# Four-index merge weights stored channel by channel, a new load order at the start, and new planner constants in a fused S4 convolution and gated-GLU kernel

## The chip, the cores and the metric

The kernel runs on one core of one Trainium2 chip. The metric is the device time of one execution in microseconds (us); lower is better. TensorE (PE) multiplies matrices, VectorE (DVE) and ScalarE (ACT) work on elements, and one queue on SyncE (SP) issues every DMA, in order. GpSimd (POOL) does nothing here.

## What is computed

`u` (2048 x 512) goes into two branches, and a gate per row mixes their results:

```python
g = _sigmoid((x * gate_w).sum(-1, keepdims=True))
# branch a: a long convolution per channel d, with a kernel K of length 2048
logdA = dt * A                     # A, B, C complex, 512 channels x 128 states
P = jnp.exp(logdA[:, :, None] * l[None, None, :])
K = jnp.einsum("dn,dnl,dn->dl", Cc, P, dB).real
y = irfft(rfft(u) * rfft(K)) + u * Dskip
# branch b: a gated linear unit, 512 -> 1792 -> 512
h = _sigmoid(x @ w_gate) * (x @ w_up)
b = h @ w_down
return g * a + (1 - g) * b
```

## The kernel before, in words

**Who orders the work.** Nothing is ordered by hand. `Plan` (L111) holds a set of generators ("strands"), one per stage. A strand yields steps (engine, assumed duration, function, what it depends on); `run` (L159) always takes the step with the smallest key, which is its possible start plus the strand's constant in `BIAS` (L49), plus a part of the cost of a change of mode (`CHANGE`, L51). The chosen step is written into the program and the plan's clocks move on. So the constants and the assumed durations fix the order of the instructions on each engine, and each engine then runs its list in that order. A buffer ("slot") is given to the next user when the plan has freed it.

**Branch b** (`load_x` L695, `load_w` L727, `split` L705, `hidden` L758, `post` L787, `down` L809, `add` L835). The rows are done in two halves of 1024, each in two tiles of 512 columns (`sb`); the 1792 hidden units are 14 blocks `f` of 128, in groups of 4, 4, 3, 3 (`GROUPS`). Every f32 operand is split into a rounded high part (ACT, L713) and a low part (DVE, L714), and three products replace one: a block needs 24 matmuls of 128x512 into `gups` (L776), then `sg` (ACT L791), the product (DVE L793), `h` high (ACT L797) and low (DVE L798). `down` multiplies a group's `h` into `dps` (L825), and `add` accumulates (L841, L845). In the first half each block is loaded in three pieces of 256 KB through the staging tiles `st` (four of them, L687), split, and also stored split to `wsp` (L754, L755); the second half reads it back from there. `gu` and `dnw` have four buffers each, and a buffer is free when the block's matmuls are done and its store has landed.

**Branch a, the kernel K.** 512 channels are 16 groups of 32. `bases` (L294) loads a group's parameters (`pg`, `dt`), makes the angles (L321 to L346) and with one exponential 21 real powers per channel (`ep`, L347): eight coarse ones, eight fine ones and five that double. The 64 merge weights `mg` of a channel are the products of coarse and fine (L353, two instructions of 1024 elements per group), the bases `bz` use the last five (L360). `tables` (L381) makes `T` by five doublings (L375 to L377) and `B` (L406 to L410), and `kps` (L427) multiplies them, 128 short matmuls. `T` and `B` have one buffer each. `first` (L436) transforms the result (`wps`, L455), evicts it (`kev`, L467) and stores two groups at a time to `a_k` (L471).

**Branch a, u and the passes.** `rows` (L482) loads 16 tiles `u` (L488), takes the gate's sum (`ju`, DVE L491), transforms (`ups`, L506), evicts and stores to `a_u` (L523). When all rows are done, the pool `early` is closed and `passes` (L541) goes through two column halves of 256: once the half's `a_k` is complete, 16 steps of `s2u`, `s2k` (L535), the products on DVE (L585 to L595), `ips` (L607), `ev` (L614) and a store to `b_s`. After the 16th step of a half, `finals` (L627) reads `b_s` back (`b_in`, L641), and eight `fps` (L654) are mixed into the output (L667, L674, with `al` loaded at L664).

Of the kernel before, what the change touches and what calls it, by code (L numbers as in the profile page):

```python
# [31 lines left out]
P = 128  # L32
# [15 lines left out]

BIAS = dict(x=-0.91, w=0.02, split=-0.1, rows=-0.2, urest=1.37, bases=0.28, tables=0.33, first=0.42, hidden=0.92,  # L49
            post=0.04, down=0.54, add=0.22, passes=-4.76, step=0.19, finals=0.41, last=0.41, const=1.21)  # L50
CHANGE = dict(ACT=0.5, PE=1)  # L51
EARLY = -0.48

# [57 lines left out]
class Plan:  # L111
# [38 lines left out]
    def cost(self, eng, n):  # L150

        if eng == "PE":
            mode, n = n
            return n + (0.1 if mode != self.last else 0.0)
        if eng == "ACT" and isinstance(n, tuple):
            return n[1] + (1.28 if n[0] != self.kind else 0.0)
        return n

    def run(self):  # L159
        while True:  # L160
# [23 lines left out]
            if eng is None:  # L184
                end = start
            elif eng == "SP":
                end = start + 0.4
                self.free[eng] = end
                self.dma = max(self.dma, end) + m / 280e3
                end = max(self.dma, end + 0.6) + 1.4  # L190
            else:
                c = self.cost(eng, m)
                self.busy[eng] = self.busy.get(eng, 0.0) + c
                end = start + c
                self.free[eng] = end
                if eng == "PE":
                    self.last = m[0]
                    end += 0.35
                else:
                    if isinstance(m, tuple):  # L200
                        self.kind = m[0]
                    end += 0.2
            fn = st[2][2]
# [5 lines left out]
def body(ctx, tc, xp, xt, prm, ldt, dsk, gw, wgu, wdn, c_wu, c_wf, c_wk, c_ww, c_pw, out):  # L209
# [84 lines left out]
    def bases():  # L294
# [3 lines left out]
        for gi in range(NG):  # L298
# [10 lines left out]
            tn = kp.tile([P, 32], I32, tag="tn", name="tn")  # L309
            ep = kp.tile([P, NP, 32], F32, tag="ep", name="ep")  # L310
            ex, mg = exs.tile("ex"), mgs.tile("mg")
# [4 lines left out]
            def first():  # L316
                V.tensor_tensor(aa, pg[:, 0:2], dg, op=OP.mult)
                V.tensor_scalar(aa[:, 1], aa[:, 1], 1 / (2 * math.pi), None, op0=OP.mult)
            t = yield "DVE", 2 * dve(64) + 0.15, first, [ta, tb]
            sh = [P, NP, 32]  # L320
            te = yield "DVE", dve(32 * NP), lambda: V.tensor_tensor(  # L321
                ep, aa[:, 0:1].to_broadcast(sh), pw[:, NA:, None].to_broadcast(sh), op=OP.mult), [t]
            t = yield "ACT", act(32), lambda: A.activation(tn, aa[:, 1], AF.Copy), [t]
# [25 lines left out]
            sh = [P, 16, 8, 8]  # L349
            m8, m1 = (ep[:, i:i + 8].rearrange("p a d -> p d a") for i in (0, 8))  # L350
            tm = max(t, te)
            for d in (slice(0, 16), slice(16, 32)):
                tm = yield "DVE", dve(1024), lambda: V.tensor_tensor(  # L353
                    mg[:, d].rearrange("p d (a b) -> p d a b", b=8), m8[:, d, :, None].to_broadcast(sh),
                    m1[:, d, None, :].to_broadcast(sh), op=OP.mult), [tm - 0.2]
            bzs, = yield BZ, 1
# [3 lines left out]
            t = yield "DVE", dve(320), lambda: V.tensor_tensor(  # L360
                bz[:, 0::2], trig, ep[:, None, 16:].to_broadcast([P, 2, 5, 32]), op=OP.mult), [t, te, bzs.t]
            ti = yield "ACT", act(160), lambda: A.activation(bz[:, 1], bz[:, 2], AF.Copy, scale=-1.0), [t]
# [3 lines left out]
    def double(dst, src, b, nd, e, t):  # L366

        n = 2 * nd * e
        sh = [P, nd, 2, e]
        slot, = yield T2, 1  # L370
        t2 = slot.tile("t2")[:, :n].rearrange("p (d c e) -> p d c e", c=2, d=nd)
        br = b[:, 0, :, None, None].to_broadcast(sh)

        sb = b[:, 1:3].rearrange("p u d -> p d u")[:, :, :, None].to_broadcast(sh)
        yield "DVE", dve(n), lambda: V.tensor_tensor(t2, src, sb, op=OP.mult), [t, slot.t]  # L375
        t = yield "DVE", dve(n), lambda: V.tensor_tensor(dst, src, br, op=OP.mult), [t]  # L376
        t = yield "DVE", dve(n), lambda: V.tensor_tensor(dst, dst, t2[:, :, ::-1], op=OP.add), [t]  # L377
        slot.free(t - 0.2)
        return t

    def tables():  # L381
        for gi in range(NG):
# [39 lines left out]
            def small():  # L422
                for s in range(8):
                    for c in range(2):
                        for jj in range(4):
                            ch = 8 * jj + s
                            mm(p[32 * jj:32 * jj + 32, s], T[:, ch, c], B[:, ch, c],  # L427
                               start=(c == 0), stop=(c == 1), tile_position=(0, 32 * jj), skip_group_check=True)
            t = yield "PE", ("128x32", 1.9), small, [t, tb, bank.t]
            tas.free(t)  # L430
# [47 lines left out]
    US, EVU, JU = (slots(ep, n, k, s) for n, k, s in (("u", 2, [P, D]), ("evu", 2, [P, 2, D]), ("ju", 1, [P, D])))  # L478
    gate = [Ev() for _ in range(NM)]
    rleft = [NM]  # L480

    def rows():  # L482
        yield E["wu"]
        yield E["gwb"]
        for t in range(NM):
            us, = yield US, 1
            u = us.tile("u")
# [15 lines left out]
            def mms():  # L503
                for jp in range(2):
                    r = slice(64 * jp, 64 * jp + 64)
                    mm(ph[jp], wu[r, jp], u[r], start=True, stop=True, tile_position=(64 * jp, 0))  # L506
            tp = yield "PE", ("64x128", 0.9), mms, [tu, E["wu"].t] + [b.t for b in banks]
            us.free(max(tp, te))
# [32 lines left out]
    def passes():  # L541

        yield E["rows"]
        early.__exit__(None, None, None)
        fp = ctx.enter_context(pool("fin"))
# [19 lines left out]
    def step(j, q, ww, wws, au, ak, s2, ta, tk):  # L565
# [37 lines left out]
        def inverse():  # L603
            for c in range(2):
                for i in range(2):
                    r = slice(64 * i, 64 * i + 64)
                    mm(pi[i], ww[r, 2 + c], y[r, c], start=(c == 0), stop=(c == 1), tile_position=(64 * i, 0))  # L607
        t = yield "PE", ("64x128", 3.4e-3 * w), inverse, [t] + [b.t for b in banks]
        ys.free(t)
# [34 lines left out]
    def last(j, m, b, s2, tb):  # L644
# [5 lines left out]
        def mms():  # L650
            for x in range(4):
                for jb in range(2):
                    r = slice(64 * jb, 64 * jb + 64)
                    mm(ph[jb][32 * x:32 * x + 32], wf[r], b[x // 2][r, x % 2], start=True, stop=True,  # L654
                       tile_position=(64 * jb, 32 * x), skip_group_check=True)
        tp = yield "PE", ("64x32", 3.4e-3 * w), mms, [tb, E["wf"].t] + [k.t for k in banks]
        for s in s2:
# [21 lines left out]
    def finished(t, te):  # L679
# [47 lines left out]
    def load_w():  # L727
        for half in range(2):
            for f in range(NF):
# [193 lines left out]
```

## Time and profile before

| what | before |
|---|---|
| median of 3 runs | 745.72 us (741.02 to 746.52) |
| the profiled execution, its own time | 748.5 us |
| its span from the first to the last instruction | 746.7 us |
| mean granted TensorE clock | 0.981 |
| busy: PE, DVE, ACT | 680.0, 590.0, 374.9 us |
| last `kps` starts | 581.1 us |
| first `s2k` of the second pass | 601.6 us |
| last `ips` starts | 700.8 us |

All times inside the execution count from the start of the span. A row of the groups gives line, engine, operation, out<-in, partitions x elements and count, then busy time and the mean of one in ns, then the idle time of the engine just before. A row of the timeline gives start, length, engine, line and what is worked on. A row of the windows gives a stretch, its length, the busy time (and count) of PE, PEld, DVE, ACT and POOL, the granted clock, the DMA share and GB/s. PE's busy time includes the modelled end of each matmul, so it is more than the matmuls' spacing.

### The profile page before, as it was taken

What the parts mean: (1) busy time and instruction counts of PE and PEld (TensorE: products, weight loads), DVE (VectorE), ACT (ScalarE), POOL (GpSimd) and SP (SyncE); (2) the same over time, 40 slices, a digit from 0 to 9 for tenths busy, and PEclk for the clock granted to TensorE, in tenths of its full rate; (3) what the DMA queues carried; (4) which work ended last, traced back from release to release, by engine and by line L of the source; (5) the groups of instructions that cost most, each with busy time, mean ns of one, the idle gap of its engine ahead of it and who ended that gap; (6) DMA issues with size and microseconds to landing.
All of it is one profiled execution on the core that took longest, in us unless ns stands there. A gap on an engine that the chain in (4) does not pass through costs nothing.

```text
span 746.7 us, 15212 instructions
## 1 busy us (share of the span) xinstructions
PE 680.0 (91%) x6176; PEld 490.9 (66%) x6176; DVE 590.0 (79%) x1043; ACT 374.9 (50%) x594; POOL 0.2 (0%) x4
## 2 busy tenths in 40 slices
PE   1979979899899999989999999999989999999986
PEld 0647657666687787867665656767757856676643
DVE  6687998989989999999998999999898334434323
ACT  4757576758746356647374737655343223222210
POOL 0000000000000000000000000000000000000000
PEclk9989999999999999999999999999999999999998
DMA  7970528771557129429357556844257465765376
GB/s 221 363 264 26 137 70 274 295 214 41 141 181 286 55 75 302 146 81 321 112 150 197 170 168 185 311 128 140 65 157 275 95 195 168 222 237 174 113 207 212
DMA packets 100486, 133.96 MB, mean 179 GB/s; under 512 B 42304, under 2 KB 65216, under 8 KB 96832
## 3 DMA queue, kind: packets, MB, share of 16 engines
q1 hardware_dynamic: 100416, 132.99, 55.8%
q8 instruction: 49, 0.80, 0.4%
q14 instruction: 21, 0.17, 0.1%
HBM read 79.48 MB, written 53.48 MB: 178 GB/s over the span
## 4 chain that ended last, share of the span: by engine, by line
PE 45%; DVE 22%; DMA 13%; ACT 12%; issue 5%; SPq 1%; DVEq 0%; ACTq 0%
PE gups L776 20%; PE dps L825 9%; DVE mg L353 6%; PE ips L607 4%; DMA au<-a_u 4%; PE s2u L535 4%; PE s2k L535 3%; DMA al<-acc 2%; DMA st<-wdn 2%; PE kps L427 2%; DVE gups L793 2%; DMA u<-xp 2%; PE ups L506 2%; ACT L345 2%; PE wps L455 1%
## 5 line engine op out<-in xcount | busy, mean ns | idle before, releaser
L776 PE MATMUL gups<-x,gu 128*128 128x512 f32 x1344 | 333.2, 399 | 4.0 <-DMA gu<-wsp 2.4
L776 PEld LDWEIGHTS gups<-x,gu 128*128 128x128 f32 x1344 | 251.7, 191 | 77.0 <-issue 18.9
L825 PE MATMUL dps<-dnw,h 128*128 128x512 f32 x672 | 178.6, 407 | 13.8 <-ACT h L797 9.1
L825 PEld LDWEIGHTS dps<-dnw,h 128*128 128x128 f32 x672 | 124.0, 191 | 61.5 <-issue 15.3
L793 DVE TENSOR_TENSOR gups<-gups,sg 128x512 f32<-128x512 f32 x56 | 39.1, 698 | 44.5 <-PE gups L776 37.8
L797 ACT ACTIVATE h<-gups 128x512 fp32r<-128x512 f32 x56 | 33.2, 593 | 74.8 <-DVE gups L793 74.8
L353 DVE TENSOR_TENSOR mg<-ep 128x1024 f32<-128x1024 f32 x32 | 65.3, 2055 | 6.7 <-ACT ep L347 6.6
L585 DVE TENSOR_TENSOR tt<-s2k,uf 128x512 f32<-128x512 f32 x32 | 22.1, 689 | 44.0 <-PE s2k L535 43.6
L791 ACT ACTIVATE sg<-gups 128x512 f32<-128x512 f32 x56 | 33.6, 599 | 33.8 <-PE gups L776 33.6
L574 ACT ACTIVATE uf<-s2u 128x512 f32<-128x512 f32 x32 | 19.0, 595 | 60.4 <-PE s2u L535 50.1
L377 DVE TENSOR_TENSOR T<-T,t 128x64 f32<-128x64 f32 (+4 forms) x80 | 46.4, 580 | 1.0
L375 DVE TENSOR_TENSOR t<-T,bz 128x64 f32<-128x64 f32 (+4 forms) x80 | 46.2, 578 | 1.2
L376 DVE TENSOR_TENSOR T<-T,bz 128x64 f32<-128x64 f32 (+4 forms) x80 | 46.1, 577 | 0.0
L845 DVE SCALAR_TENSOR_TENSOR acc<-dps,omg,acc 128x512 f32<-128x512 f32 x48 | 36.0, 749 | 10.7 <-PE dps L825 10.6
L798 DVE TENSOR_TENSOR h<-gups,h 128x512 fp32r<-128x512 f32 x56 | 38.6, 688 | 6.7 <-ACT h L797 6.5
L427 PE MATMUL kps<-B,T 128*32 128x64 f32 x2048 | 33.7, 225 | 7.5 <-ACT evu L517 5.1
L535 PE MATMUL s2u<-au,ww 128*64 128x256 f32 x256 | 34.6, 390 | 6.4 <-DMA au<-a_u 5.5
L614 ACT ACTIVATE ev<-ips 128x256 f32<-128x256 f32 x64 | 21.0, 381 | 38.6 <-PE ips L607 38.5
L467 ACT ACTIVATE kev<-wps 128x256 f32<-128x256 f32 x64 | 33.2, 665 | 14.3 <-PE wps L455 14.2
L427 PEld LDWEIGHTS kps<-B,T 128*32 128x32 f32 x2048 | 31.0, 114 | 13.5 <-issue 6.1
L506 PE MATMUL ups<-u,wu 64*128 64x512 f32 x64 | 23.8, 734 | 17.0 <-DMA u<-xp 15.3
L406 DVE TENSOR_TENSOR B<-ex,mg 128x1024 f32<-128x1024 f32 x32 | 38.2, 1219 | 0.0
(80 smaller groups left out, 717.5 us busy)
## 6 DMA issues: line engine op xcount, KB each, us to landing
wsp<-gu SPq DMA_DIRECT2D x14, 1024.0 KB, 6.6
gu<-wsp SPq DMA_DIRECT2D x14, 1024.0 KB, 8.6
a_u<-evu SPq DMA_DIRECT2D x32, 256.0 KB, 4.0
a_k<-kev SPq DMA_DIRECT2D x8, 1024.0 KB, 6.8
ww<-c_ww SPq DMA_DIRECT2D x32, 256.0 KB, 3.0
au<-a_u SPq DMA_DIRECT2D x32, 256.0 KB, 3.5
ak<-a_k SPq DMA_DIRECT2D x32, 256.0 KB, 4.6
b_s<-ev SPq DMA_DIRECT2D x32, 256.0 KB, 4.7
```

The lines of the kernel that those rows point to most:

```text
L353: tm = yield "DVE", dve(1024), lambda: V.tensor_tensor(mg[:, d].rearrange("p d (a b) -> p d a b", b=8), m8[:, d, :, None].to_broadcast(sh) ...
L375: yield "DVE", dve(n), lambda: V.tensor_tensor(t2, src, sb, op=OP.mult), [t, slot.t]
L376: t = yield "DVE", dve(n), lambda: V.tensor_tensor(dst, src, br, op=OP.mult), [t]
L377: t = yield "DVE", dve(n), lambda: V.tensor_tensor(dst, dst, t2[:, :, ::-1], op=OP.add), [t]
L406: yield "DVE", dve(1024), lambda: V.tensor_tensor(B[:, d, :, 32:], ex[:, d, :, :32], mg[:, d, None, 32:].to_broadcast(sh), op=OP.mult), [tb]
L427: mm(p[32 * jj:32 * jj + 32, s], T[:, ch, c], B[:, ch, c], start=(c == 0), stop=(c == 1), tile_position=(0, 32 * jj), skip_group_check=True)
L506: mm(ph[jp], wu[r, jp], u[r], start=True, stop=True, tile_position=(64 * jp, 0))
L535: mm(p[64 * kb_:64 * kb_ + 64, c], ww[:, kb_, 64 * c:64 * c + 64], a(kb_), start=True, stop=True, tile_position=(0, 64 * kb_), skip_group_ ...
L776: mm(p, gu[:, a, k, dc], x[:, b, dc], start=(dc + n == 0), stop=(dc == NC - 1 and n == 2))
L793: t = yield "DVE", dve(512), lambda: V.tensor_tensor(pu, pu, sg, op=OP.mult), [t, tu]
L798: t = yield "DVE", dve(512), lambda: V.tensor_tensor(h[:, 1], pu, h[:, 0].bitcast(F32), op=OP.subtract), [t]
L825: mm(p, h[:, a, 128 * s:128 * s + 128], dn[:, b], start=(f == f0 and n == 0), stop=(f == f0 + gn - 1 and n == 2))
```

## The change

Line numbers in this section's new lines are three to ten higher than before's.

- `ep` is stored as [channel][power] instead of [power][channel]. `mg` then reads its coarse weight with eight repeats and its fine weights as eight neighbours; before, neighbours of the innermost index lay 32 elements apart. The product that makes `ep` (L321) and `bz` (L360) read their operands the other way round accordingly.
- A tile of `u` is not planned to be loaded before 8.7 + 12.1 t us on the plan's clock (`PACE`).
- The four loads of x's second tile wait until the weights of block 3 are issued (`XLATE`).
- Four more staging tiles lie in the pool `early`; `passes` takes them before it closes the pool.
- `BIAS`, `CHANGE`, `EARLY` and some assumed durations and latencies are other numbers. The assumed duration of one `mg` instruction, 1.13 us, is the same.

```diff
-CHANGE = dict(ACT=0.5, PE=1)
-EARLY = -0.48
+CHANGE = dict(ACT=0.5, PE=2)
+XLATE = 3
+PACE = [8.7, 12.1]
+EARLY = 0.5
...
-            ep = kp.tile([P, NP, 32], F32, tag="ep", name="ep")
+            ep = kp.tile([P, 32, NP], F32, tag="ep", name="ep")
...
-            sh = [P, NP, 32]
+            sh = [P, 32, NP]
             te = yield "DVE", dve(32 * NP), lambda: V.tensor_tensor(
-                ep, aa[:, 0:1].to_broadcast(sh), pw[:, NA:, None].to_broadcast(sh), op=OP.mult), [t]
+                ep, aa[:, 0, :, None].to_broadcast(sh), pw[:, None, NA:].to_broadcast(sh), op=OP.mult), [t]
...
             sh = [P, 16, 8, 8]
-            m8, m1 = (ep[:, i:i + 8].rearrange("p a d -> p d a") for i in (0, 8))
+            m8, m1 = ep[:, :, 0:8], ep[:, :, 8:16]
...
             t = yield "DVE", dve(320), lambda: V.tensor_tensor(
-                bz[:, 0::2], trig, ep[:, None, 16:].to_broadcast([P, 2, 5, 32]), op=OP.mult), [t, te, bzs.t]
+                bz[:, 0::2], trig, ep[:, :, 16:].rearrange("p d k -> p k d")[:, None].to_broadcast([P, 2, 5, 32]), op=OP.mult), [t, te, bzs.t]
...
+    more = slots(ep, "se", 4, [P, 512])
...
         for t in range(NM):
+            yield None, 0.0, None, [PACE[0] + PACE[1] * t]
             us, = yield US, 1
...
         yield E["rows"]
+        yield more, len(more)
         early.__exit__(None, None, None)
...
+    ST += more
...
-    wstored = [Ev() for _ in range(NF)]
+    wstored, begun_w = [Ev() for _ in range(NF)], [Ev() for _ in range(NF)]
...
             for sb in range(2):
+                if (half, sb) == (0, 1):
+                    yield begun_w[XLATE]
                 xsl, = yield X_, 1
...
                     yield from split(wdn[f], dn[:, 0], dn[:, 1], *args)
+                    begun_w[f].set(0.0)
```

The new constants move instructions on every engine. Three places matter below.

DVE, from the last instruction on `steps` (which makes the step sizes) to the first instruction of group 0 of K (`aa`). Before, in part:

```order
L282 TENSOR_TENSOR steps<-steps 16x32
L714 TENSOR_TENSOR x<-st,x 128x512
L714 TENSOR_TENSOR gu<-st,gu 128x512
L714 TENSOR_TENSOR x<-st,x 128x512
L491 SCALAR_TENSOR_TENSOR ju,gl<-u,gwb 128x512
L714 TENSOR_TENSOR x<-st,x 128x512
L517 COPY evu<-ups 128x512
L714 TENSOR_TENSOR x<-st,x 128x512 x3
L491 SCALAR_TENSOR_TENSOR ju,gl<-u,gwb 128x512
...
L491 SCALAR_TENSOR_TENSOR ju,gl<-u,gwb 128x512
L317 TENSOR_TENSOR aa<-pg,dt 128x64
```

Now:

```order
L285 TENSOR_TENSOR steps<-steps 16x32
L723 TENSOR_TENSOR x<-st,x 128x512
L723 TENSOR_TENSOR gu<-st,gu 128x512 x2
L723 TENSOR_TENSOR dnw<-st,dnw 128x512
L723 TENSOR_TENSOR gu<-st,gu 128x512 x2
L723 TENSOR_TENSOR dnw<-st,dnw 128x512
L723 TENSOR_TENSOR gu<-st,gu 128x512 x2
L723 TENSOR_TENSOR dnw<-st,dnw 128x512
L320 TENSOR_TENSOR aa<-pg,dt 128x64
```

The second tile of x and the work on `u` have left this place; ten splits stand ahead of `aa`, all but one of weights.

PE, from the last `kps` to the first step of the second pass (`s2u`). Before:

```order
L427 MATMUL kps<-B,T 32x64 x64
L455 MATMUL wps<-wk,kst 64x64 x32
L776 MATMUL gups<-x,gu 128x512 x18
L455 MATMUL wps<-wk,kst 64x64 x32
L825 MATMUL dps<-dnw,h 128x512 x30
L776 MATMUL gups<-x,gu 128x512 x12
L535 MATMUL s2u<-au,ww 64x256 x4
```

Now:

```order
L430 MATMUL kps<-B,T 32x64 x64
L835 MATMUL dps<-dnw,h 128x512 x3
L786 MATMUL gups<-x,gu 128x512 x6
L458 MATMUL wps<-wk,kst 64x64 x32
L786 MATMUL gups<-x,gu 128x512 x24
L835 MATMUL dps<-dnw,h 128x512 x3
L786 MATMUL gups<-x,gu 128x512 x18
L540 MATMUL s2u<-au,ww 64x256 x4
```

The `wps` of the group before the last now stands ahead of the last `kps`, and 9 matmuls of branch b instead of 18 and a `wps` stand between the last `kps` and its own `wps`.

PE, the end of the program. Before:

```order
L825 MATMUL dps<-dnw,h 128x512 x12
L654 MATMUL fps<-b_in,wf 32x256 x8
L825 MATMUL dps<-dnw,h 128x512 x6
L654 MATMUL fps<-b_in,wf 32x256 x8
L825 MATMUL dps<-dnw,h 128x512 x12
L654 MATMUL fps<-b_in,wf 32x256 x8
```

Now:

```order
L786 MATMUL gups<-x,gu 128x512 x6
L660 MATMUL fps<-b_in,wf 32x256 x8
L786 MATMUL gups<-x,gu 128x512 x6
L660 MATMUL fps<-b_in,wf 32x256 x8
L835 MATMUL dps<-dnw,h 128x512 x30
```

The last 30 matmuls of `down` now follow the last `fps`. From the last `ips` to the end stand 150 matmuls of branch b, before 102. Ahead of the last `kps` stand 1614, before 1650. Ahead of the fourth `kps`, in turn, stand 537, before 474.

On SP the four loads of x's second tile now follow the twelve loads of blocks 0 to 3, the eight stores of these blocks follow, and then the first tile of `u`. Nine tiles of `u` come after the second batch of weight loads, before three.

More of the change, by code (lines that the diff above doesn't have):

```diff
@@ L46 @@
 BANKS = dict(gu=3, dn=2, xb=3)
-BIAS = dict(x=-0.91, w=0.02, split=-0.1, rows=-0.2, urest=1.37, bases=0.28, tables=0.33, first=0.42, hidden=0.92,
-            post=0.04, down=0.54, add=0.22, passes=-4.76, step=0.19, finals=0.41, last=0.41, const=1.21)
-CHANGE = dict(ACT=0.5, PE=1)
-EARLY = -0.48
+BIAS = dict(x=-3.75, w=0.38, split=0.4, rows=-0.13, urest=1.21, bases=0.28, tables=0.35, first=0.47, hidden=0.91,
+            post=0.08, down=0.69, add=0.25, passes=-1.77, step=0.28, finals=0.11, last=0.24, const=4.74)
+CHANGE = dict(ACT=0.5, PE=2)
+XLATE = 3
+PACE = [8.7, 12.1]
+EARLY = 0.5
 def constants():
@@ L153, in cost @@
             mode, n = n
-            return n + (0.1 if mode != self.last else 0.0)
+            return n + (0.0 if mode == self.last else 0.09 if self.last == "f" else 0.1)
         if eng == "ACT" and isinstance(n, tuple):
@@ L186, in run @@
             elif eng == "SP":
-                end = start + 0.4
+                end = start + 0.43
                 self.free[eng] = end
@@ L197, in run @@
                     self.last = m[0]
-                    end += 0.35
+                    end += 0.22
                 else:
@@ L201, in run @@
                         self.kind = m[0]
-                    end += 0.2
+                    end += 0.13
             fn = st[2][2]
@@ L354, in bases @@
                     mg[:, d].rearrange("p d (a b) -> p d a b", b=8), m8[:, d, :, None].to_broadcast(sh),
-                    m1[:, d, None, :].to_broadcast(sh), op=OP.mult), [tm - 0.2]
+                    m1[:, d, None, :].to_broadcast(sh), op=OP.mult), [tm - 0.13]
             bzs, = yield BZ, 1
@@ L377, in double @@
         t = yield "DVE", dve(n), lambda: V.tensor_tensor(dst, dst, t2[:, :, ::-1], op=OP.add), [t]
-        slot.free(t - 0.2)
+        slot.free(t - 0.13)
         return t
@@ L428, in small @@
                                start=(c == 0), stop=(c == 1), tile_position=(0, 32 * jj), skip_group_check=True)
-            t = yield "PE", ("128x32", 1.9), small, [t, tb, bank.t]
+            t = yield "PE", ("128x32", 1.83), small, [t, tb, bank.t]
             tas.free(t)
@@ L506, in mms @@
                     mm(ph[jp], wu[r, jp], u[r], start=True, stop=True, tile_position=(64 * jp, 0))
-            tp = yield "PE", ("64x128", 0.9), mms, [tu, E["wu"].t] + [b.t for b in banks]
+            tp = yield "PE", ("64x128", 0.96), mms, [tu, E["wu"].t] + [b.t for b in banks]
             us.free(max(tp, te))
@@ L607, in inverse @@
                     mm(pi[i], ww[r, 2 + c], y[r, c], start=(c == 0), stop=(c == 1), tile_position=(64 * i, 0))
-        t = yield "PE", ("64x128", 3.4e-3 * w), inverse, [t] + [b.t for b in banks]
+        t = yield "PE", ("64x128", 3.75e-3 * w), inverse, [t] + [b.t for b in banks]
         ys.free(t)
@@ L655, in mms @@
                        tile_position=(64 * jb, 32 * x), skip_group_check=True)
-        tp = yield "PE", ("64x32", 3.4e-3 * w), mms, [tb, E["wf"].t] + [k.t for k in banks]
+        tp = yield "PE", ("64x32", 0.5 / 256 * w), mms, [tb, E["wf"].t] + [k.t for k in banks]
         for s in s2:
```

## The prediction

> **What bounds the kernel now.** I read the page first, then the windows by stage, then who waits ahead of `kps`. On the page:
>
> ```profile
> span 746.7 us, 15212 instructions
> PE 680.0 (91%) x6176; PEld 490.9 (66%) x6176; DVE 590.0 (79%) x1043; ACT 374.9 (50%) x594; POOL 0.2 (0%) x4
> PE   1979979899899999989999999999989999999986
> DVE  6687998989989999999998999999898334434323
> ```
>
> PE looks like the bound, but its busy time counts modelled ends. DVE's 79% is an average too: its slices stand at 8 and 9 up to three quarters of the span and fall to 3 behind that. The windows, cut where the work changes, say the same:
>
> ```profile
> 0.00:75.00 75.00, 54.01 (x246) 37.73 (x250) 53.81 (x112) 46.45 (x74) 0.20 (x4) 0.95 0.63 218
> 75.00:561.00 486.00, 454.92 (x4611) 337.37 (x4603) 454.95 (x781) 288.31 (x435) 0.00 (x0) 0.99 0.54 170
> 602.00:705.00 103.00, 101.06 (x594) 66.74 (x590) 44.95 (x84) 26.23 (x60) 0.00 (x0) 1.00 0.56 183
> 705.00:746.70 41.70, 31.40 (x218) 19.04 (x216) 14.08 (x26) 2.99 (x5) 0.00 (x0) 0.91 0.67 202
> ```
>
> From 75 to 561 us DVE is busy 454.95 of 486 us, and PE as long: 31 us idle each. Which of them leads is seen where they meet, at the `kps`:
>
> ```profile
> 253.01 1.24 DVE T L377
> 254.38 2.00 PE kps L427 x128
> ...
> 579.41 1.22 DVE L377 TENSOR_TENSOR T<-T,t 128x1024 f32<-128x1024 f32 x1
> 581.12 1.99 PE L427 MATMUL kps<-B,T 128*32 128x64 f32 x128
> ...
> L427 PE MATMUL kps<-B,T x2048: 216/219/314, 74.3 to 582.9; 128*32 128x64 f32 x187
> ```
>
> `kps` starts within 0.1 and 0.5 us of the end of the doubling that it needs (253.01 + 1.24 and 579.41 + 1.22). PE has matmuls of branch b to fill in, and K waits for DVE. The sixteen `kps` run from 74.3 to 581.1, so 33.8 us a group, and after the last of them comes a tail that nothing shortens by itself: store `a_k`, 16 steps, finals. So the end is the time of the last `kps` plus the tail, and DVE sets the first, with PE close behind.
>
> **The change part by part.** The merge weights first, with the instructions nearest to their old and new forms; the number behind the busy time is the mean of one in ns.
>
> ```profile
> L353 DVE TENSOR_TENSOR mg<-ep 128x1024 f32<-128x1024 f32 x32 | 65.3, 2055 | 6.7 <-ACT ep L347 6.6
> L409 DVE TENSOR_TENSOR B<-mg,ex 128x1024 f32<-128x1024 f32 x16 | 19.5, 1218 | 0.0
> L376 DVE TENSOR_TENSOR T<-T,bz 128x128 f32<-128x128 f32 x16 | 4.6, 287 | 0.0
> L337 DVE TENSOR_TENSOR w<-pg,dt 128x64 f32<-128x64 f32 x16 | 3.5, 219 | 0.0
> L394 DVE TENSOR_TENSOR w<-w,ex 128x64 f32<-128x64 f32 x16 | 4.4, 274 | 0.6
> L375 DVE TENSOR_TENSOR t<-T,bz 128x64 f32<-128x64 f32 x16 | 4.2, 264 | 0.0
> L321 DVE TENSOR_TENSOR ep<-aa,pw 128x672 f32<-128x672 f32 x16 | 13.6, 850 | 0.0
> L360 DVE TENSOR_TENSOR bz<-ex,ep 128x320 f32<-128x320 f32 x16 | 11.6, 728 | 0.0
> L594 DVE TENSOR_TENSOR y<-tt 128x256 f32<-128x256 f32 x32 | 13.4, 420 | 0.0
> ```
>
> `mg` and L409 both make 1024 elements from two f32 tiles in SBUF, and L353 costs 837 ns more. What differs is the step: in L353 the fine weights lie 32 elements apart. L394 shows the same at 64 elements (one operand 76 elements apart): 274 against 219 ns in L337, 0.86 ns per element, against 0.82 here. The new `mg` reads runs of eight neighbours; L376's form of 128 elements has runs of two and already costs 287, no more than the straight line from 219 (64 elements) to 420 (256) gives, 286. So I price it at 1.22 us, bounds 1.22 and 2.055. That is 32 x 0.837 = 26.8 us less on DVE, all of it ahead of the last `kps`.
>
> `bz` now reads both operands with steps. L360 already pays for one: a plain instruction of 320 elements costs some 487 by the line from 420 at 1.05 ns per element, it takes 728. L375 at 64 elements steps in both of its inputs and costs 264, less than one step in L394. So I take 0; the upper bound is the same penalty again, 16 x 0.24 = 3.8 us. The Trainium skill, SBUF — State Buffer, section "Door 1: The DMA port swizzle", says that each access to a new 16-byte line pays; taken as one payment for each operand it would give those 3.8 us, and the trace's L375 does not show the second payment. `ep` changes which operand repeats, and `mg`'s own case is the only one where such a pattern was dear; its new innermost run is 21 neighbours, so 850 stays. `ep`'s exponential runs over the same 672 neighbours either way.
>
> How much of 26.8 us reaches the end? PE must do the same work in fewer us. By the count in the order, 36 matmuls fewer stand ahead of the last `kps`; at 7.10 us for 30 (below) that is 8.5 us less. The stretch from 75 shrinks by 27 to 459 us with 446 us of PE in it, 97% busy; 101.06 of 103 us in the second pass is 98%, so it can be done, but hardly a stall may be left. PE's share was 93.6% (454.92 of 486). I take the middle of that and 98%, 96%: 446 / 0.96 = 465, so 6 us are lost again. The bounds are 0 (at 98%) and 17 (at 93.6%, 476 us).
>
> The start:
>
> ```profile
> 10.40 0.18 DVE L282 TENSOR_TENSOR steps<-steps 16x32 f32<-16x32 f32 x1
> 12.74 2.08 PE L506 MATMUL ups<-u,wu 64*128 64x512 f32 x4 [12.74 <-DMA u<-xp]
> 19.34 5.91 PE L776 MATMUL gups<-x,gu 128*128 128x512 f32 x18
> 24.58 0.22 DVE L317 TENSOR_TENSOR aa<-pg,dt 128x64 f32<-128x64 f32 x1
> L714 DVE TENSOR_TENSOR gu<-st,gu 128x512 fp32r<-128x512 f32 x28 | 18.7, 687 | 4.2 <-ACT gu L713 4.0
> ```
>
> K's first instruction, `aa`, came at 24.58. Now ten splits stand between the end of `steps` (10.58) and `aa`: 10 x 0.687 = 6.9 us, so 17.5 if the loads keep up, which eight staging tiles instead of four are for. That is 7 us earlier on DVE. PE begins with `gups` near 13 instead of two tiles of `u`, but the first `kps` stands behind 39 matmuls more (9.2 us) and 6 `ups` less (0.52 each by the row, 3.1). I take 5 us of gain, bounds 0 and 8. What is late instead are the tiles of `u`: nothing needs `a_u` before the first pass, when eight groups of K are done.
>
> The tail:
>
> ```profile
> 588.45 1.16 PE L455 MATMUL wps<-wk,kst 64*64 64x64 f32 x64
> 589.54 7.10 PE L825 MATMUL dps<-dnw,h 128*128 128x512 f32 x30
> 601.60 1.08 PE L535 MATMUL s2k<-ak,ww 128*64 128x256 f32 x8 [0.30 <-DMA ak<-a_k]
> 700.79 1.13 PE L607 MATMUL ips<-y,ww 64*128 64x256 f32 x8
> 704.75 5.33 SPq L641 DMA_DIRECT2D b_in<-b_s  x8
> 734.59 2.56 SPq L641 DMA_DIRECT2D b_in<-b_s  x4
> 738.71 1.53 PE L654 MATMUL fps<-b_in,wf 64*32 64x256 f32 x16
> ```
>
> The last `wps` began 5.3 us after the end of the last `kps` (583.11). Now 9 matmuls, 2.1 us, stand between them: 3.2 us less for everything behind. The 16 steps (601.6 to 700.8, 6.2 us each, with DMAs to and from DRAM in each) hold 198 matmuls of branch b, before 204: no change. The finals are bound by SP, which issues nearly without a pause from 704.75 to 737.15; PE is busy 31.40 of 41.70 us there, so the 48 matmuls more after the last `ips` fill idle time. But 30 of them now follow the last `fps`: 7.1 us, then the last sum and its store, where before the sum came right behind `fps`. Against that, one store less stands ahead of the last `b_in`, and the first of these 30 may overlap what `fps` waited for. I take +5, bounds 0 and +7.
>
> On the profiled execution: 748.5 - 26.8 + 6 - 5 - 3.2 + 5 = 724.5. That execution was 2.8 us above the median of the runs, so **721 us** in terms of the median, with the fraction dropped. Its own range, halfway to the bounds and all pulling together, is 714 (3 less lost, 1.5 more at the start, 2.5 less at the end) to 730 (5.5 more lost, 2.5 less at the start, 1 more at the end).
>
> **Rivals.** *DVE's other idle time goes too* (707): the 31 us that DVE idles from 75 on are partly waits for PE, whose order no longer runs into late tables; if 8 of them vanish and the 6 us above are not lost, 721 - 14. For it: L353 took 2.055 us where the plan assumed 1.13, so the plan reckoned with each table 1.8 us too early. Against: PE has no room for it, 97% being reckoned already.
>
> *PE paces* (739): if PE could not go faster, the relief of DVE is swallowed, and only the 36 matmuls that leave (8.5), the `wps` (3.2) and the end (+5) count: 748.5 - 6.7 - 2.8. For it: PE idles no more than DVE from 75 to 561. Against: the two rows of `kps` above.
>
> *The weights don't get cheaper* (742): if the price of `mg` hangs on its four indices with two repeats and not on the step, it stays at 2.055: 748.5 - 5 - 3.2 + 5 - 2.8. L375, L376 and L394 speak against it. The Trainium skill, VectorE: DVE Perf Modes, section "Mode 1× (REGULAR) — the baseline", goes this way: that mode assumes nothing, odd strides and f32 included, and gives one result per cycle. By that rule the layout is worth nothing; the trace disagrees, with 2055 against 1218 ns.
>
> *The tiles of u hold up PE* (753, slower). SP issues in order, and nine tiles of `u` now come after the second batch of weights, six more than before. There, stores to `wsp` stand ahead of them, which wait for splits, which wait for buffers; a late tile stops PE at its `ups`, and all matmuls behind.
>
> ```profile
> 158.83 8.78 DMA u<-xp
> PE ups L506 <- DMA u<-xp: 15.3, 2, 12.7
> ```
>
> The chain of before has one such load of 8.78 us. If six more cost PE 5.3 us each, 32 us, the gain is gone: 721 + 32. From about 4 us each the time is that of before. Against: PE waited 15.3 us in all for `u`, 12.7 of that at the very start, and two buffers let a load go ahead.
>
> **How the numbers follow.** Forecast 0.65, idle time goes too 0.13, PE paces 0.12, weights no cheaper 0.04, `u` holds up PE 0.06. A measurement of this kernel tells about 1%, 7.5 us, from no change, so faster means under 738.3: forecast, the first rival and half of the second, 0.84; within 1%: the other half and the third, 0.10; slower 0.06. The range, 702 to 739, holds the forecast, nearly all of the first rival and half of the second.
>
> **What would show it.** Right: `mg` near 1.22 us and `bz` near 0.73; `aa` near 17.5 us; the last `kps` near 555 us, still right behind its doubling; some 17 us from there to the first `s2k` of pass two; 42 to 49 us from the first `b_in` of pass two to the end. Wrong: `mg` above 1.5 us; or `kps` starting many us after its doubling (PE paces); or PE idle ahead of `ups` between 100 and 250 us, for more than 20 us in all. If the last `kps` comes after 570 us, the forecast fails whatever the total.

## The result, and the profile after

| what | before | after |
|---|---|---|
| median of 4 runs each | 745.18 us | 723.96 us (719.10 to 727.08) |
| ratio after / before | | 0.972 [0.965, 0.979] |
| the profiled execution, its own time | 748.5 us | 727.08 us |
| its span | 746.7 us | 725.3 us |
| first `kps` starts | 74.3 us | 66.0 us |
| last `kps` starts | 581.1 us | 554.9 us |
| first `s2k` of the second pass | 601.6 us | 573.3 us |
| last `ips` starts | 700.8 us | 670.7 us |

21 us are gone; 721 were forecast. First the page's totals and two of its rows of slices:

```profile
span 725.3 us, 15192 instructions
PE 678.0 (93%) x6176; PEld 491.3 (68%) x6176; DVE 567.9 (78%) x1045; ACT 374.6 (52%) x592; POOL 0.2 (0%) x4
PE   3999999999799969989999998998999999999987
DVE  6698999898999999898999998997996444443233
```

DVE did 22 us less than before, PE 2 us less. (Two copies of `evu` more run on DVE and take 1.3 us of its gain back.) The groups by form name the instruction that DVE's share comes from, and one that became dearer (mean ns behind the busy time):

```profile
L356 DVE TENSOR_TENSOR mg<-ep 128x1024 f32<-128x1024 f32 x32 | 38.3, 1220 | 4.1 <-ACT ep L350 4.0
L363 DVE TENSOR_TENSOR bz<-ex,ep 128x320 f32<-128x320 f32 x16 | 13.1, 821 | 0.0
L412 DVE TENSOR_TENSOR B<-mg,ex 128x1024 f32<-128x1024 f32 x16 | 19.5, 1220 | 0.0
```

`mg` went from 2055 to 1220 ns, to the ns what L412 takes, which also makes 1024 elements. `bz`, which now steps in both inputs, went from 728 to 821 ns.

The windows from the first `kps` to the end of the last, over the second pass, and over the finals (columns as before: stretch, length, busy time and count of PE, PEld, DVE, ACT, POOL, then clock, DMA share, GB/s):

```profile
66.00:557.00 491.00, 465.60 (x4979) 343.50 (x4979) 451.77 (x819) 295.16 (x455) 0.00 (x0) 0.98 0.57 184
573.00:672.00 99.00, 97.03 (x575) 63.26 (x576) 43.72 (x82) 24.18 (x56) 0.00 (x0) 1.00 0.56 187
672.00:725.30 53.30, 45.72 (x278) 30.58 (x277) 18.59 (x32) 5.20 (x10) 0.00 (x0) 0.97 0.51 163
```

Over the stretch of K, PE is the busier of the two: 94.8%, DVE 92.0%. Taken over the whole stretch, from the first `kps` to the end of the last, it was so before as well, 93.7% against 92.9%:

```profile
74.30:583.00 508.70, 476.42 (x4977) 353.96 (x4976) 472.69 (x815) 293.79 (x445) 0.00 (x0) 0.99 0.55 173
```

`kps` follows its doubling closely, as the timeline shows for the last group (start, length):

```profile
553.55 1.22 DVE L380 TENSOR_TENSOR T<-T,t 128x1024 f32<-128x1024 f32 x1
554.93 1.99 PE L430 MATMUL kps<-B,T 128*32 128x64 f32 x128
559.12 1.16 PE L458 MATMUL wps<-wk,kst 64*64 64x64 f32 x64
```

The doubling ends at 554.77, `kps` starts 0.16 us later, and the `wps` 2.2 us after `kps` has ended. Over the sixteen groups the first of these distances is 0.06 to 3.15 us, 1.1 in the mean; before it was 0.15 to 3.20, 1.2 in the mean. That alone does not show who waits. PE's idle time ahead of `kps`, in the groups of before and of after (the last part of each row), does:

```profile
L427 PE MATMUL kps<-B,T 128*32 128x64 f32 x2048 | 33.7, 225 | 7.5 <-ACT evu L517 5.1 <-DVE T L377 1.1 <-issue 0.9
L430 PE MATMUL kps<-B,T 128*32 128x64 f32 x2048 | 33.8, 225 | 7.4 <-DVE T L380 6.2
```

PE stood idle for the doubling 1.1 us in all before and 6.2 us after. At thirteen of the sixteen `kps` before, and at eleven after, it came straight from other matmuls.

The finals took longer than before, 54.6 us from the last `ips` against 45.9. SP's rows in the timeline of after, with the `o` that its stores wait for, the last matmuls and the last sum:

```profile
674.66 5.22 SPq L647 DMA_DIRECT2D b_in<-b_s  x8
...
687.66 2.90 SPq L677 DMA_DIRECT2D out<-o  x2
...
693.61 0.48 DVE L673 SCALAR_TENSOR_TENSOR o<-fps,g,al 128x256 f32<-128x256 f32 x1 [0.27 <-DMA al<-acc]
...
694.28 2.40 SPq L677 DMA_DIRECT2D out<-o  x2
...
696.73 0.42 SPq L670 DMA_DIRECT2D al<-acc  x1
697.24 2.55 SPq L647 DMA_DIRECT2D b_in<-b_s  x4
699.10 0.48 DVE L673 SCALAR_TENSOR_TENSOR o<-fps,g,al 128x256 f32<-128x256 f32 x1 [5.00 <-DMA al<-acc]
...
699.85 0.58 SPq L670 DMA_DIRECT2D al<-acc  x1
...
700.53 3.29 SPq L677 DMA_DIRECT2D out<-o  x2
702.97 0.48 DVE L673 SCALAR_TENSOR_TENSOR o<-fps,g,al 128x256 f32<-128x256 f32 x1 [2.72 <-DMA al<-acc]
...
708.67 2.56 SPq L647 DMA_DIRECT2D b_in<-b_s  x4
...
712.34 1.78 PE L660 MATMUL fps<-b_in,wf 64*32 64x256 f32 x16
714.05 7.49 PE L835 MATMUL dps<-dnw,h 128*128 128x512 f32 x30
721.57 0.75 DVE L855 SCALAR_TENSOR_TENSOR acc<-dps,omg,acc 128x512 f32<-128x512 f32 x1 [1.29 <-PE dps L835]
```

Two pairs of stores in the timeline of before, with what SP issues between them:

```profile
718.52 0.86 SPq L671 DMA_DIRECT2D out<-o  x2
...
719.43 0.93 SPq L664 DMA_DIRECT2D al<-acc  x2
...
720.46 2.55 SPq L641 DMA_DIRECT2D b_in<-b_s  x4
...
723.11 1.01 SPq L671 DMA_DIRECT2D out<-o  x2
```

A pair of stores held SP for 0.86 to 1.01 us before; now three of them hold it for 2.40 to 3.29 us. The cause for two of them, at 687.66 and 700.53, is SP's order. Before, it issues two `al`, then four `b_in`, then the two stores: the `al` land and the `o` are made largely while the `b_in` are issued. Now it issues one `al`, four `b_in`, one `al` and then the two stores: the second `al` stands directly ahead of the pair (699.85), `o` waits for it until 702.97, and the second store waits for that `o`. SP's waits for `o` over the loads of `b_in`, in before and in after (us in total, times, longest):

```profile
SPq L671 <- DVE o L667: 0.5, 1, 0.5
```

```profile
SPq L677 <- DVE o L673: 4.6, 2, 2.5
```

For the pair at 694.28 both `o` were made by 694.09, so it is something else that held SP there, and I do not know what. The next `al` and `b_in` stand behind each pair. From the first to the end of the last `b_in` it was 32.4 us and is 36.6; from there to the end 9.55 and now 14.07, and there the 30 matmuls are PE's last work.

### The profile page after: what moved, and what is told of

The parts are those of the page before. It is cut to its first block, busy times and chain, and to the rows that moved or that the text cites. A ratio compares the mean times of both kernels' runs of the same rounds, so it can differ in the third digit from the quotient of the medians.

```text
span 725.3 us, 15192 instructions
## 1 busy us (share of the span) xinstructions
PE 678.0 (93%) x6176; PEld 491.3 (68%) x6176; DVE 567.9 (78%) x1045; ACT 374.6 (52%) x592; POOL 0.2 (0%) x4
## 4 chain that ended last, share of the span: by engine, by line
PE 72%; DMA 10%; DVE 9%; ACT 4%; SPq 3%; issue 3%; DVEq 0%; ACTq 0%
PE gups L786 35%; PE dps L835 16%; DMA au<-a_u 4%; PE ips L613 4%; PE kps L430 4%; PE s2u L540 4%; PE s2k L540 3%; DMA u<-xp 3%; PE wps L458 2%; PE ups L511 2%; PE fps L660 2%; ACT kev L470 1%; DMA a_k<-kev 1%; DVE t L378 1%; DVE T L379 1%
## 5 line engine op out<-in xcount | busy, mean ns | idle before, releaser
L835 PE MATMUL dps<-dnw,h 128*128 128x512 f32 x672 | 176.7, 405 | 1.4 <-ACT h L807 0.9
L620 ACT ACTIVATE ev<-ips 128x256 f32<-128x256 f32 x64 | 21.4, 380 | 42.3 <-PE ips L613 42.3
L470 ACT ACTIVATE kev<-wps 128x256 f32<-128x256 f32 x64 | 33.5, 669 | 17.5 <-PE wps L458 17.4
L356 DVE TENSOR_TENSOR mg<-ep 128x1024 f32<-128x1024 f32 x32 | 38.3, 1220 | 4.1 <-ACT ep L350 4.0
L430 PE MATMUL kps<-B,T 128*32 128x64 f32 x2048 | 33.8, 225 | 7.4 <-DVE T L380 6.2
L613 PE MATMUL ips<-y,ww 64*128 64x256 f32 x256 | 36.3, 402 | 0.1
```

The lines of the kernel that those rows point to most:

```text
L356: tm = yield "DVE", dve(1024), lambda: V.tensor_tensor(mg[:, d].rearrange("p d (a b) -> p d a b", b=8), m8[:, d, :, None].to_broadcast(sh) ...
L430: mm(p[32 * jj:32 * jj + 32, s], T[:, ch, c], B[:, ch, c], start=(c == 0), stop=(c == 1), tile_position=(0, 32 * jj), skip_group_check=True)
L470: te = yield "ACT", 0.95, lambda: [A.activation(dst[:, :, i], src[:, :, i], AF.Copy) for i in range(2)], [t, kv.t]
L835: mm(p, h[:, a, 128 * s:128 * s + 128], dn[:, b], start=(f == f0 and n == 0), stop=(f == f0 + gn - 1 and n == 2))
```

## The experiments

Each ratio goes by runs of the kernel before on the same chip (its medians were 745.2 to 747.4 us); four runs of each kernel (old_layout seven), and the `kps` are those of the profiled one. "Ahead of the last `kps`" counts the matmuls of branch b that PE's order has there; behind it I give those after the last `kps`, the last `ips` and the last `fps`.

| kernel | median us | ratio [95%] | first / last `kps` | ahead; behind |
|---|---|---|---|---|
| before | 745.2 | 1 | 74.3 / 581.1 | 1650; 366, 102, 0 |
| after | 723.96 | 0.972 [0.965, 0.979] | 66.0 / 554.9 | 1614; 402, 150, 30 |
| new_layout | 731.0 | 0.980 [0.975, 0.984] | 71.9 / 566.6 | as before |
| old_layout | 740.7 | 0.995 [0.991, 0.999] | 68.4 / 571.1 | as after |
| less_dve | 724.5 | 0.969 [0.964, 0.975] | 66.9 / 552.3 | as after |
| less_pe | 722.5 | 0.969 [0.964, 0.974] | 64.0 / 549.6 | as after, but 1502 ahead |
| less_both | 715.1 | 0.960 [0.957, 0.963] | 63.7 / 543.9 | as after, but 1502 ahead |
| no_pace | 731.8 | 0.979 [0.973, 0.985] | 66.4 / 562.6 | 1614; 402, 150, 30 |
| no_more | 776.3 | 1.043 [1.036, 1.049] | 68.9 / 555.6 | 1422; 594, 327, 192 |
| no_xlate | 782.4 | 1.050 [1.045, 1.054] | 66.6 / 560.5 | 1422; 594, 327, 192 |
| old_consts | 780.4 | 1.049 [1.041, 1.056] | 81.9 / 626.6 | 1884; 132, 0, 0 |
| tail_act | 721.9 | 0.970 [0.967, 0.973] | 66.2 / 556.7 | as after |
| tail_pool | 726.0 | 0.974 [0.969, 0.979] | 67.3 / 556.3 | as after |
| wide_tail | 722.4 | 0.968 [0.964, 0.973] | 66.7 / 557.5 | as after |

**Layout and order apart.** *new_layout* is the kernel before with the five edits of the layout alone; *old_layout* is the changed kernel with them undone. The instructions of each engine stand in the order of before and of after.

```diff
-            ep = kp.tile([P, NP, 32], F32, tag="ep", name="ep")
+            ep = kp.tile([P, 32, NP], F32, tag="ep", name="ep")
...
-            m8, m1 = (ep[:, i:i + 8].rearrange("p a d -> p d a") for i in (0, 8))
+            m8, m1 = ep[:, :, 0:8], ep[:, :, 8:16]
```

> The kernel before with the new layout of ep alone, the order on every engine as before. DVE paces K: about 18 us less than 745, so 727, last kps near 562, and the rest of the gain belongs to the order. PE paces, or the gain is the new order's: 740 to 745.

> The changed kernel with ep in the layout of before, every engine's instructions in the same order as in the changed kernel. DVE paces K: mg is back at 2.055 us, 26.8 us more on DVE, of which 18 to 25 reach the end, so 724 + 21 = about 745, last kps near 577; bz falls from 0.821 to 0.728. PE paces: the time stays within 6 us of 724. The new order is what counts: also within 6 us of 724.

The groups by form of new_layout:

```profile
L353 DVE TENSOR_TENSOR mg<-ep 128x1024 f32<-128x1024 f32 x32 | 38.5, 1219 | 5.2 <-ACT ep L347 5.1
L360 DVE TENSOR_TENSOR bz<-ex,ep 128x320 f32<-128x320 f32 x16 | 13.1, 818 | 0.0
```

The same two of old_layout:

```profile
L356 DVE TENSOR_TENSOR mg<-ep 128x1024 f32<-128x1024 f32 x32 | 65.5, 2073 | 4.1 <-ACT ep L350 4.0
L363 DVE TENSOR_TENSOR bz<-ex,ep 128x320 f32<-128x320 f32 x16 | 11.7, 734 | 0.0
```

Both prices go with the layout, whatever the order. The layout alone brings 2.0% (1.6 to 2.5), 15 us; the order alone 0.5% (0.1 to 1.0), 4 us. The first `kps` comes 2.4 us earlier by the layout and 5.9 by the order, together the 8.3 of after; the last comes 14.5 us earlier by the layout, 10.0 by the order, 26.2 by both. Behind the last `kps` the order costs: 165.6 us to the end before, 164.1 in new_layout, 167.8 and 170.4 in old_layout and after. So most of the gain is the layout's; the order brings K forward and gives part of it back at the end. Both kernels went the way of the first theory, by less than it said: the last `kps` at 566.6 and not near 562, and at 571.1 and not near 577.

**Which engine holds K now.** Three kernels leave work out of after, in the slots where it stood: *less_dve* the last, longest sum of the doublings (16 x 1.22 us), *less_pe* one of three products of `down` in the first half (112 matmuls counted, some 25 us), *less_both* both.

```diff
-        t = yield "DVE", dve(n), lambda: V.tensor_tensor(dst, dst, t2[:, :, ::-1], op=OP.add), [t]
+        t = yield "DVE", dve(n), lambda: V.tensor_tensor(dst, dst, t2[:, :, ::-1], op=OP.add) if e < 16 else None, [t]
...
-                                for n, (a, b) in enumerate(((0, 0), (1, 0), (0, 1))):
+                                parts = ((0, 0), (1, 0), (0, 1))[:3 - (half == 0)]
+                                for n, (a, b) in enumerate(parts):
```

> The changed kernel without the addition that ends the last doubling of T, one DVE instruction of 1.22 us per group, 19.5 us in all; what is computed is then not K. DVE still paces: the last kps comes 12 to 18 us earlier than 554.9 and the time is 709 to 713. PE paces by now: the last kps moves by less than 6 us and the time is above 718.

> The changed kernel without one of three products in the first half's down projection, 112 matmuls of 0.227 us less on PE, 25 us, all ahead of the last kps; half of the rows then lack that product. DVE paces: the last kps comes at most 8 us earlier and the time is 716 to 724. PE paces: the last kps comes 15 to 25 us earlier and the time is 700 to 709.

> Both of the last two cuts in one kernel: 19.5 us less on DVE and 25 us less on PE ahead of the last kps (K lacks the last addition of T, half of the rows lack one product). The two engines share the pace and each alone was held by the other: the last kps comes 14 to 20 us earlier than 554.9 and the time is 704 to 711. Something else paces (ScalarE, the latency of a chain through all engines, the DMA queue): it stays above 718, as each cut alone did.

Windows over the stretch of K, of less_dve:

```profile
67.00:554.00 487.00, 464.19 (x4973) 341.13 (x4975) 434.68 (x804) 294.77 (x454) 0.00 (x0) 0.99 0.58 185
```

of less_pe:

```profile
64.00:551.00 487.00, 449.07 (x4856) 325.84 (x4858) 450.50 (x819) 295.29 (x455) 0.00 (x0) 0.98 0.58 185
```

and of less_both:

```profile
64.00:546.00 482.00, 446.23 (x4875) 322.81 (x4864) 434.63 (x804) 294.60 (x455) 0.00 (x0) 0.98 0.58 188
```

Taking 19.5 us from DVE alone brought the last `kps` 2.6 us forward, taking 25 us from PE alone 5.3; neither total can be told from after's, and the 2.6 us are hardly more than two executions of one order differ by (up to 2.5 us, below under the finals). Taking both brought 11.0 us, and this interval lies wholly under after's. So neither engine alone holds K: where one is relieved the other stands right behind. In less_dve the won time is seen ahead of `kps`: from the last instruction of the doubling to `kps` it takes 3.0 us in the mean, in after 1.1, and PE is at other matmuls meanwhile. The widest case, the tenth group:

```profile
356.20 1.22 DVE L379 TENSOR_TENSOR T<-T,bz 128x1024 f32<-128x1024 f32 x1
...
363.94 1.99 PE L430 MATMUL kps<-B,T 128*32 128x64 f32 x126
```

But 11 of some 20 us is not all either, and under the 14 to 20 that were expected. In less_both PE is busy 92.6% of the stretch and DVE 90.2%, both less than in after, so a part goes into waits between the two that a fixed order keeps.

**The other pieces.** *no_pace* loads `u` when the plan has a buffer, *no_more* does without the four staging tiles, *no_xlate* does not hold x's second tile back; the constants stay. *old_consts* has the structure of after with before's `BIAS`, `CHANGE`, `EARLY`, durations and latencies.

```diff
-            yield None, 0.0, None, [PACE[0] + PACE[1] * t]
...
-    more = slots(ep, "se", 4, [P, 512])
...
-        yield more, len(more)
...
-    ST += more
...
-                if (half, sb) == (0, 1):
-                    yield begun_w[XLATE]
```

And of old_consts, a part:

```diff
-CHANGE = dict(ACT=0.5, PE=2)
+CHANGE = dict(ACT=0.5, PE=1)
-EARLY = 0.5
+EARLY = -0.48
...
-                end = start + 0.43
+                end = start + 0.4
```

> The changed kernel without the set intervals for u. PE's order hardly differs (the counts ahead of the kps are within 9 matmuls of the changed kernel's). The pace is worth nothing by itself: 721 to 728. The even spacing of u is what keeps PE fed early: first kps later than 68 and 730 or more.

> The changed kernel without the four extra staging tiles. The order then puts 1422 matmuls ahead of the last kps and leaves 192 behind the last fps, as in the kernel with x's second tile at its old place. DVE bounds K from below: the last kps comes no earlier than 545 in spite of 44 us less work for PE ahead of it, and the time is 765 to 790, since PE ends last. PE paces K: the last kps comes near 515.

> The changed kernel with x's second tile loaded at its old place, ahead of most of the first weights; the planner then orders everything anew. The start's gain comes from this part: the first kps moves from 66.0 towards 72 and the time is 728 to 732. The start's gain comes from the paced u and the staging: the first kps stays within 2 us of 66 and the time within 4 us of 724.

> The changed kernel's layout, staging, pace and late second tile of x, with all planner constants of before. The order then puts 1884 matmuls of branch b ahead of the last kps and not 1614. PE holds K too: 270 matmuls of 0.227 us are 61 us, the last kps comes at 600 to 616, and with a tail of 160 the time is 760 to 778. DVE alone paces K, as the forecast had it: the last kps stays within 10 us of 555 and the time is 715 to 730.

The windows of no_more, from the first `kps` to the end of the last, and from there to the end:

```profile
69.00:557.50 488.50, 444.31 (x4837) 324.28 (x4836) 438.11 (x800) 288.49 (x444) 0.00 (x0) 0.95 0.55 172
560.00:772.80 212.80, 199.87 (x1120) 139.72 (x1111) 77.24 (x135) 40.34 (x84) 0.00 (x0) 1.00 0.52 168
```

The same two of old_consts:

```profile
82.00:628.50 546.50, 517.56 (x5195) 386.76 (x5195) 462.39 (x831) 301.09 (x456) 0.00 (x0) 0.98 0.51 166
628.00:776.70 148.70, 105.69 (x752) 59.93 (x740) 48.74 (x96) 26.08 (x59) 0.00 (x0) 0.83 0.58 177
```

These two show the balance from its ends. In no_more the plan put 192 matmuls fewer ahead of the last `kps`, some 45 us of PE, and it came at 555.6 all the same, so less work for PE does not bring it forward. That DVE holds it there is not shown: PE is busy 91.0% of that stretch and DVE 89.7%, both less than in after. The 192 then run behind the last `fps`, PE is busy 94% of the last 213 us, and the end comes 52 us later. In old_consts 270 more stand ahead, PE is busy 94.7% up to the end of the last `kps` and DVE 84.6%, K waits for PE until 626.6, and behind it PE idles 43 of 149 us. That went the way expected, but further (600 to 616 was expected, and 760 to 778 in all). After stands between the two, with 1614 ahead.

no_xlate gave the matmul counts of no_more and nearly its time, which neither theory expected; what it did settle is that the first `kps` stayed (66.6), so the earlier start does not need x's second tile held back. no_pace met neither expectation: the first `kps` stayed at 66.4, but the last came 7.7 us later, and 6 us of that were lost between the third and the fourth (134.7 to 176.9 us, in after 132.8 to 169.0). These two stretches of no_pace and of after:

```profile
134.70:176.90 42.20, 40.77 (x280) 26.31 (x280) 38.28 (x72) 29.23 (x54) 0.00 (x0) 1.00 0.48 128
```

```profile
132.80:169.00 36.20, 35.92 (x326) 25.09 (x326) 33.33 (x62) 26.87 (x45) 0.00 (x0) 1.00 0.34 92
```

Little of that is waiting: DVE and PE each do 5 us more there, since eight tiles of `u` fall into the stretch and in after five. The interval of no_pace overlaps that of after. In all these kernels the plan makes a new order under constants that stood beside the piece; their times price that order, not the piece.

**The finals.** *tail_act* puts the loads of `al` and the stores of `o` on ACT's queue, *tail_pool* on GpSimd's, *wide_tail* is tail_act with three buffers for each of the two.

```diff
-                ta = yield "SP", kb(w / 2), lambda: S.dma_start(al, acc0[t, :, cols]), [als.t, stored[t].t]
+                ta = yield "SP", kb(w / 2), lambda: A.dma_start(al, acc0[t, :, cols]), [als.t, stored[t].t]
...
-                os_.free((yield "SP", kb(w / 2), lambda: S.dma_start(out[t, :, cols], o), [te]))
+                os_.free((yield "SP", kb(w / 2), lambda: A.dma_start(out[t, :, cols], o), [te]))
```

> The changed kernel, the loads of al and the stores of o in the finals issued by ScalarE's queue and not by SP's. SP's order holds up the finals of pass two (it stands at stores that wait for results, with loads of b_in behind them): 36.6 us from the first to the last b_in become 24 to 30, the time falls by 5 to 9 us to about 717. The finals are bound by the loads' own time or by PE's order: within 3 us of 724.

> The same with GpSimd's queue, where nothing else runs that such a wait could hold up. SP's order holds up the finals: 715 to 719, as on ScalarE's queue or some us better, for the first pass's finals too. PE's order or the loads bind: within 3 us of 724.

> The changed kernel with al and o on ScalarE's queue and with three buffers each and not two, so that a load or a store waits less for an earlier one. The finals wait for these buffers: first to last b_in of pass two from 33.8 us (queue alone) to under 30 and the time about 717. PE's own order holds the finals (150 matmuls are left behind the last ips): 720 to 724, no better than the queue alone.

SP in the timeline of tail_act:

```profile
675.26 29.98 SPq L647 DMA_DIRECT2D b_in<-b_s  x28
...
706.49 2.56 SPq L647 DMA_DIRECT2D b_in<-b_s  x4
```

From the first to the end of the last `b_in` it took 33.8 us in tail_act, 34.6 in tail_pool, 32.7 in wide_tail, against 36.6 in after and 32.4 before. So 2 to 4 of the 4.2 us that were added there come back when `al` and `o` leave SP, which takes away SP's waits at the stores and also the time to issue these transfers; 24 to 30 us were expected for the stretch. What remains is not SP alone: the 28 loads stand in its queue with nothing between them and still take 30 us. Its waits there for `fps` to release a buffer, which in after are 0.7 us:

```profile
SPq L647 <- PE fps L660: 7.3, 6, 2.8
```

From the last `kps` to the end tail_act and wide_tail took 166.3 and 165.0 us, after 170.4; but their last `kps` came 1.8 and 2.5 us later. Of that, 1.4 and 2.2 us are there at the thirteenth `kps` (463.05 us in after, 464.46 and 465.22 in these), ahead of the first instruction that the edits touch (at 488 us); so executions of one order differ by that much. The totals cannot be told from after's. None of the kernels that do the whole work is measurably faster than after.

## Why the prediction came out right, and which term was off

The forecast was 721 us, the median 723.96: the cause and the main terms hold, and the finals were off.

| step, us on the profiled execution | predicted | measured |
|---|---|---|
| `mg` | -26.8 | -26.7 (32 x 0.835) |
| `bz` | 0 (to +3.8) | +1.5 (16 x 0.093) |
| lost again between first and last `kps` | +6 (0 to 17) | +5.7 |
| start | -5 (0 to -8) | -6.7 |
| last `kps` to first `s2k` | -3.2 | -2.1 |
| 16 steps | 0 | -1.8 |
| last `ips` to the end | +5 (0 to +7) | +8.7 |
| sum | -24.0 | -21.4 |

How the measured column is made: the first `kps` came 8.3 us earlier, of which 1.6 are group 0's own `mg` and `bz` and counted in the first two rows. From first to last `kps` the stretch shrank by 17.9 us; 15 of the 16 groups lie in it and got 23.6 us cheaper, so 5.7 were lost again. The terms missed by 6.4 us the one way and by 3.8 us the other, so that the sum is off by only 2.6 us is in part luck.

- **The weights** are right in cause and size, and the rival in which they stay dear is out: old_layout and new_layout move the price with the layout alone. The rule cited there from the Trainium skill, VectorE: DVE Perf Modes, section "Mode 1× (REGULAR) — the baseline", one result per cycle with odd strides included, by which the layout is worth nothing, does not hold here: 2055 against 1220 ns.
- **`bz`** was taken as free because L375 at 64 elements showed no second payment. At 320 elements there is one, 93 ns, against some 240 for the first step. Read as one payment per operand, the note in the Trainium skill, SBUF — State Buffer, section "Door 1: The DMA port swizzle", gave 3.8 us in all; 1.5 were measured, so neither reading holds.
- **The 6 us lost again** came out as 5.7, but partly by luck: its working used a window that ended 22 us before the end of the last `kps`, and over the whole stretch PE's share is 94.8%, not the 96% reckoned. The reason given, that PE must do the same work in less time, is borne out: with the layout alone PE's share of its stretch rose from 93.7% to 95.5%, and further relief of DVE alone brings nothing that can be told (less_dve). I had DVE in the lead with PE close behind, from two `kps` that start 0.1 and 0.5 us behind their doubling. That was not enough to say so: over all sixteen PE stood idle for the doubling only 1.1 us, and over the whole stretch PE was the busier already before. Measured, neither leads alone.
- **The start**: `aa` came at 18.68 us, 1.51 of it waiting for `dt`'s load; the forecast 17.5 had no such wait. On PE the working counted six `ups` fewer ahead of the first `kps`; it is twelve (20 before, 8 now); at 0.52 us each that is an estimated 3.1 us more, which makes up for the wait. The last `kps` to the first `s2k` took 18.4 us, where some 17 were forecast.
- **The finals** are the term that was off, and the step that failed is the one on SP: that it "issues nearly without a pause" and that one store less ahead of the last `b_in` could only help. SP's order was read for how many stores stand ahead of the last `b_in`, not for where each `al` stands and which store waits for it. From the first `b_in` to the end it took 50.6 us, and 42 to 49 were forecast; the term came out at +8.7, past its bound of +7. Two costs of like size make it up: +4.2 us up to the last `b_in`, against 4.1 us more that SP waits for `o`, and +4.5 behind it, where 30 matmuls follow the last `fps` as forecast.
- **Rivals**: *the tiles of u hold up PE* fell; the waits of PE on `u` between 66 and 555 us, from the table of waits (us in total, times, longest), beside the longest that K causes:

```profile
PE kps L430 <- DVE T L380: 6.2, 2, 5.5
...
PE ups L511 <- DMA u<-xp: 4.4, 2, 3.0
```

*DVE's other idle time goes too* fell, as the 39 us that DVE idles in the window show (36 before, over the whole stretch). *PE paces* was wrong as put, since the relief of DVE was not swallowed; less_pe and less_both show how near it was.

## What to carry to other kernels

Price an operand's step from the nearest rows of the same trace: the same 1024 elements took 2055 ns with neighbours 32 elements apart and 1220 ns in runs of eight. Where two engines are both over 90% busy, saved time is paid only in part, here 15 of 25 us with the order kept, and only relieving each alone and then both tells how near the second one stands. When a plan makes a new order, count for each engine what stands ahead of and behind the last instruction of the critical stage, and read the end of every in-order queue again: what is brought forward in the middle can be given back there. A load that stands directly ahead of the store that needs it holds the queue until it has landed, here 4.6 us at two stores; with four other loads between, the waits were 0.5 us in all.

## What the hardware showed that was not expected

- The payment for a step is not the same for each operand: 320 f32 elements took 728 to 734 ns with one stepping input and 818 to 821 with two, in four kernels. At 64 elements two stepping inputs (264 ns) cost no more than one (274).
- The granted clock in the window of old_consts behind the last `kps` is 0.83, where PE is busy 71% of the time; in after's windows with PE at 86 to 98% it is 0.97 to 1.00. What sets it was not tried.
